# A transformer block on one core: the order of work for three engines taken from a list written in the kernel, and attention's small matmuls regrouped

## The chip, the cores and the metric

The kernel runs on one core of a Trainium2 chip. The metric is the time of one execution on the device in microseconds (us). Engines are named as in the profile: PE (TensorE) for matmuls, PEld for its weight loads, DVE (VectorE), ACT (ScalarE), POOL (GpSimd), SP (SyncE, which only issues DMAs). Each engine works through its own instructions in order.

## What is computed

A sequence of 2048 tokens of width 1024, in bfloat16, goes through an attention sublayer and a gated MLP, each behind a layer norm and with a residual. Attention has 32 heads of 32, and each token attends to 8 positions: itself and those 2, 4, ... 14 tokens earlier.

```python
h  = x + A(_layernorm(x), A_wqkv, A_wo)
h2 = h + B(_layernorm(h), B_w_in, B_w_sp, B_b_sp, B_w_out)

def A(x, wqkv, wo):              # B, S, D = x.shape; H, Dh, W, dil = 32, 32, 8, 2
    q, k, v = split(x @ wqkv)
    idx = pos[:, None] - (arange(W) * dil)[None, :]
    logits = einsum('bhsd,bhswd->bhsw', q, k[idx]) * Dh ** -0.5   # masked where idx < 0
    return einsum('bhsw,bhswd->bhsd', softmax(logits), v[idx]) @ wo

def B(x, w_in, w_sp, b_sp, w_out):    # Fh = 1792
    z = gelu(x @ w_in)
    z1, z2 = z[..., :Fh], _layernorm(z[..., Fh:])
    g = einsum('ts,bsf->btf', w_sp, z2) + b_sp[None, :, None]
    return (z1 * g) @ w_out
```

## The kernel before, in words

The tokens are cut into four chunks of 512 (`CH`), a chunk into four tiles of 128. A first phase computes, chunk by chunk, everything up to z1 and z2; a second phase (from L494 on, untouched by the change) mixes over all tokens with `w_sp` (L511), gates, and multiplies by `w_out` (L528, L536). The second phase needs z2 of all four chunks.

The first phase has, for a chunk c:

- The first layer norm: `stats` (L140 to L144) and `norm` (L162) on DVE, a square root on ACT (L157). Chunk 0 is transposed on PE (`xpose`, L170). Chunks 1 to 3 are written to DRAM (`xn_d`, L193) and come back transposed by a DMA (`xnT`, L221).
- `qkv(c)`: 192 matmuls of 128x512 on PE (L230, L238) into PSUM tiles `acc`, of which there are three; ACT copies each out (L242, L245). Chunks 1 to 3 go through DRAM (`qkv_d`) and are read back by POOL's DMAs (L257 to L259).
- `attention(c)`: head and feature lie across partitions, so the dot products run on DVE. For each of the 8 offsets w, DVE multiplies q by the shifted k (`prod`, L266), halves the 8 slices three times by adding (L268, L270, L272), and PE sums within heads by four small matmuls with a constant `E32` (L275) into one PSUM tile `L`. Then come the softmax (L280 to L291, with the exponential on ACT at L285), and four groups of eight small matmuls with a constant `B4` (L299, tile `pb`) that spread the weights back over the partitions, copied out by ACT (L300). Eight multiplications with the shifted v (L306, L309) and seven additions (L310) give `oT`.
- `b_head(c)`: for each tile, two matmuls with an identity bring the residual `xr` into PSUM (L346; not in chunk 3), 16 matmuls multiply `oT` by `wo` (L349). ACT copies out and sums for the second layer norm (L360, L361; in chunk 3 DVE does it, L354 to L358). `batch_rstd` (L313 to L326) works out mean and inverse deviation with a square root on ACT (L322). ACT normalises (L374), and a DMA transposes into `hnT` (L375); chunk 3 is transposed on PE (L384).
- `b_z2(c)`: per tile 28 matmuls (L405), gelu on ACT (L407), squares on ACT (L414), then a layer norm whose last step is on DVE (L423). `b_z1(c)`: 112 matmuls (L435) and gelu (L438).

What sets the order. The calls stand in the order qkv(0), qkv(1), attention(0), qkv(2), b_head(0), attention(1), qkv(3), b_head(1), then per chunk b_z2, b_z1, the head of the next chunk and the attention of the one after. The framework then sorts each engine's instructions by priority (the order of the code) and by when its own model finds them ready; `high_priority` blocks (L273, L284, L294) go ahead. `NWARM` = 14 matmuls on zeros (L125) run at the start while the inputs load. Tiles come from pools with a number of buffers; a new tile waits until the last reader of the buffer that it takes over is done.

## Time and profile before

| what | value |
|---|---|
| median of 6 runs | 765.97 us (762.57 to 766.83) |
| profiled execution: its time | 766.83 us |
| profiled execution: span from first to last instruction | 765.0 us |
| busy PE / DVE / ACT / POOL | 741.7 / 437.3 / 232.5 / 20.7 us |
| mean granted PE clock | 0.991 |

A row of a group reads: line, engine, operation, what it writes and reads, shape, count, then busy time in us and the mean ns of one, then the idle time of the engine just before these instructions and what ended it. Matmuls overlap in the pipeline, so the mean ns of one is longer than the distance between two. A few matmul records are missing, so counts of a group can fall short of the code's.

### The profile page before, as it was taken

The page shows a single profiled execution, that of the slowest core. Times are in us where ns is not written, and L with a number is a line of the kernel's source. Part 1 is how long each engine was busy: PE and PEld are TensorE (multiplying, and loading weights), DVE is VectorE, ACT ScalarE, POOL GpSimd, SP SyncE. Part 2 cuts the span into 40 slices and gives each one's busy share as a digit, 9 for nine tenths or more (in the row PEclk, how much of TensorE's full clock was granted, in tenths as well). Part 3 has the DMA queues.
Part 4 walks back from the last instruction along what each step waited for, and adds up shares of the span by engine and source line. Part 5 has one row for each costly group of instructions (what it writes and reads, how often), then busy time and mean ns, then how long its engine had stood idle before and what let it go on. Part 6 is the DMA issues. An engine that isn't in the chain of part 4 may idle for free.

```text
span 765.0 us, 8765 instructions
## 1 busy us (share of the span) xinstructions
PE 741.7 (97%) x3622; PEld 378.2 (49%) x3686; DVE 437.3 (57%) x445; ACT 232.5 (30%) x297; POOL 20.7 (3%) x32
## 2 busy tenths in 40 slices
PE   7999999999989998999999999999999999999997
PEld 3666666546634544444545544444444444444443
DVE  4889699989999799988945010332232222222322
ACT  3322433257328944686652562000000000000000
POOL 0000000000000000000003000000000000000000
PEclk8999999999999999999999999999999999999999
DMA  9984453174892742244047968517201711020001
GB/s 343 331 245 113 146 159 126 57 212 114 294 315 86 154 179 72 74 160 124 1 165 293 216 225 210 170 42 179 69 29 43 185 61 42 27 83 28 1 18 65
DMA packets 109640, 104.33 MB, mean 136 GB/s; under 512 B 63536, under 2 KB 87376, under 8 KB 109472
## 3 DMA queue, kind: packets, MB, share of 16 engines
q1 hardware_dynamic: 103120, 76.89, 33.4%
q0 software_dynamic: 6192, 26.36, 10.2%
q8 instruction: 29, 0.48, 0.3%
q10 hardware_dynamic: 288, 0.52, 0.2%
q14 instruction: 11, 0.09, 0.0%
HBM read 55.19 MB, written 33.88 MB: 116 GB/s over the span
## 4 chain that ended last, share of the span: by engine, by line
PE 70%; DVE 22%; ACT 4%; issue 3%; DMA 0%; DVEq 0%; ACTq 0%
PE acc L511 25%; PE acc L528 12%; PE acc L435 9%; PE acc L238 8%; PE acc L405 6%; DVE oT L310 6%; DVE prod L309 6%; PE acc L349 5%; DVE prod L266 3%; DVE scq L268 2%; PE acc L230 1%; DVE oT L306 1%; DVE scq L270 1%; PE acc L536 1%; DVE u L423 1%
## 5 line engine op out<-in xcount | busy, mean ns | idle before, releaser
L511 PE MATMUL acc<-wspT,z2sb 128*128 128x512 bf16 x878 | 193.1, 379 | 0.9
L511 PEld LDWEIGHTS <-z2sb 128*128 128x128 bf16 x896 | 87.7, 98 | 105.7
L514 DVE TENSOR_TENSOR g<-acc,bB 128x1024 bf16<-128x1024 f32 x28 | 34.3, 1225 | 159.7 <-PE acc L511 134.5
L435 PE MATMUL acc<-hnT,win 128*128 128x512 bf16 x448 | 99.6, 379 | 0.7 <-ACT z1s L438 0.7
L405 PE MATMUL acc<-win,hnT 128*128 128x512 bf16 (+1 forms) x500 | 98.1, 352 | 0.8 <-ACT u L407 0.2
L266 DVE TENSOR_TENSOR prod<-qT,kT 128x4096 bf16<-128x4096 bf16 x32 | 73.1, 2285 | 2.3 <-ACT kT L242 2.2
L405 PEld LDWEIGHTS <-hnT 128*128 128x128 bf16 x512 | 49.5, 98 | 46.6 <-issue 0.4
L435 PEld LDWEIGHTS <-win 128*128 128x128 bf16 x448 | 43.2, 98 | 50.7 <-issue 0.9
L528 PEld LDWEIGHTS <-zg 128*128 128x128 bf16 x420 | 41.1, 98 | 49.5
L309 DVE TENSOR_TENSOR prod<-vT,AB 128x4096 bf16<-128x4096 bf16 x28 | 64.2, 2291 | 1.3
L310 DVE TENSOR_TENSOR oT<-oT,prod 128x4096 bf16<-128x4096 bf16 x28 | 64.2, 2292 | 0.8
L349 PE MATMUL acc<-wo_sb,oT 128*128 128x512 bf16 x251 | 60.0, 385 | 0.5 <-issue 0.2
L245 ACT CAST stg<-acc 128x1024 bf16<-128x1024 f32 x36 | 36.4, 1013 | 77.9 <-PE acc L238 75.0
L238 PE MATMUL acc<-xnT,wv 128*128 128x512 bf16 x250 | 59.1, 388 | 0.5 <-issue 0.2
L530 DVE TENSOR_TENSOR ot<-acc,hr 128x1024 bf16<-128x1024 f32 x15 | 18.4, 1225 | 69.4 <-PE acc L528 60.5
L238 PE MATMUL acc<-xnT,wk 128*128 128x512 bf16 x252 | 56.4, 380 | 0.2
L528 PE MATMUL acc<-wout_a,zg 128*128 128x512 bf16 x236 | 54.0, 379 | 0.3
L238 PE MATMUL acc<-xnT,wq 128*128 128x512 bf16 x217 | 50.0, 380 | 0.4
L238 PEld LDWEIGHTS <-wk 128*128 128x128 bf16 x256 | 36.6, 144 | 18.2
L238 PEld LDWEIGHTS <-wv 128*128 128x128 bf16 x256 | 36.2, 145 | 18.9 <-issue 2.1
L528 PE MATMUL acc<-wout_b,zg 128*128 128x512 bf16 x175 | 40.7, 379 | 0.2
L407 ACT ACTIVATE u<-acc 128x1024 bf16<-128x1024 f32 (+1 forms) x32 | 29.3, 916 | 34.4 <-PE acc L405 34.4
(110 smaller groups left out, 535.4 us busy)
## 6 DMA issues: line engine op xcount, KB each, us to landing
qkv_d<-stg SPq DMA_DIRECT2D x36, 256.0 KB, 2.6
z_d<-z1s SPq DMA_DIRECT2D x28, 256.0 KB, 2.6
z1c<-z_d SPq DMA_DIRECT2D x28, 256.0 KB, 2.9
z_d<-u SPq DMA_DIRECT2D x12, 448.0 KB, 3.3
z2sb<-z_d POOLq DMA_DIRECT2D x12, 448.0 KB, 8.5
xr<-in_A_x_dram SPq DMA_DIRECT2D x16, 256.0 KB, 2.9
h_d<-hb SPq DMA_DIRECT2D x16, 256.0 KB, 2.8
win<-in_B_w_in_dram POOLq DMA_DIRECT2D x2, 2048.0 KB, 12.0
```

Source lines behind the costliest of these rows:

```text
L238: T.matmul(acc[:, j, :], wv[:, kt, dl, :], xnT[c][:, kt, :], start=(kt == 0), stop=(kt == KT - 1))
L245: A.copy(stg[:], acc[:])
L266: V.tensor_tensor(prod[:], qT[:], kT[:, :, o:o + CH], op=ALU.mult)
L309: V.tensor_tensor(prod[:], vT[:, :, o:o + CH], abb, op=ALU.mult)
L310: V.tensor_tensor(oT[:], oT[:], prod[:], op=ALU.add)
L349: T.matmul(acc[:, nh, :], oT[:, dl, il * P:(il + 1) * P], wo_sb[:, dl, nh * CH:(nh + 1) * CH], start=(last and dl == 0), stop=(dl == DLO - 1))
L405: T.matmul(accf[:, n0:n1], hnT[:, il, kt, :], wt[:, kt, n0:n1], start=(kt == 0), stop=(kt == KT - 1))
L407: A.activation(u[:, hf * 1024:hf * 1024 + wd], accf[:, 0:wd], ACTF.Gelu_apprx_tanh, accum_out=sums[:, il, hf:hf + 1])
L435: T.matmul(acc[:, j, :].rearrange("p (a b) -> p a b", a=TPC), wt[:, kt, f0 * P:(f0 + 1) * P], hnT[:, :, kt, :], start=(kt == 0), stop=(kt ...
L511: T.matmul(acc[:, j, :], z2sb[a][:, f * P:(f + 1) * P], wspT[:, a, :], start=(a == 0), stop=(a == NT - 1))
L514: V.tensor_tensor(g1[:], acc[:], bB[:, c * CH:(c + 1) * CH].unsqueeze(1).to_broadcast([P, 2, CH]), op=ALU.add)
L528: T.matmul(acc[:, nh, :], zg[:, f, il * P:(il + 1) * P], wt[:, f0, nh * CH:(nh + 1) * CH], start=(f == 0), stop=(f == NF - 1))
```

## The change

Everything that was called in order in the first phase is now entered as operations into a list, `Order`, each with its engine, an assumed duration, what it depends on, a priority (low goes first), and which PSUM or SBUF slots it takes and frees. `Order.run` simulates the engines, picks at each step the engine that can start earliest and on it the operation of best priority, and then emits the code in the order of the simulated starts. PE, ACT and DVE keep exactly that order (`manual_schedule`); SP and POOL are still sorted by the framework. Priorities on PE: attention's small matmuls 1, the matmuls of `head` 4, and qkv, z2 and z1 6 with a running number, so all of qkv(0) to qkv(3) comes before z2(0), z1(0), z2(1) and so on.

The work itself changes in these places:

- Attention: the second and third additions are left to PE. With `LMODE` 2 (chunks 0 and 1) one DVE addition (L270's) stays and L272's goes; with 4 (chunks 2 and 3) both go. PE sums the remaining 2 or 4 slices by accumulating matmuls of 512 or 256 columns, in 2 or 4 groups per chunk, in place of 8 groups of four with 128 columns. In the simulation every group but the last waits `LSLACK` = 1 us beyond its operands; `BSLACK` does the same for the second half of the spreading matmuls below.
- Softmax: subtraction, exponential, sum and scaling are cut into two halves. The spreading matmuls are two of 512 columns per group, with 32 rows of `B4` each, in place of eight of 128 columns; half of the groups use an `acc` buffer, and DVE copies out one of the four.
- `head`: the identity matmuls are gone. DVE adds the residual while it copies out and sums (`scalar_tensor_tensor`), ACT squares. `batch_rstd` takes the inverse root on POOL by a power of -0.5.
- z2 of chunks 0 to 2 is normalised on ACT (`Z2ACT`).
- `NWARM` is 20; x, u, stg, z1s and the normalised x share buffers (`x4k`, four of 4 KB per partition, and `xn`, six); `wo` is loaded ahead of the list; x is loaded in the same order as before.

The core of the diff:

```diff
-NWARM = 14
+NWARM = 20
+XRB = 3
+LMODE = (2, 2, 4, 4)
+LSLACK, BSLACK = 1.0, 1.0
+Z2ACT = (4, 4, 4, 0)
...
+class Order:
...
+    def add(self, eng, us, fn, deps=(), prio=5.0, lat=0.1, take=None, free=None, table=None):
+        o = _Op()
+        o.eng, o.us, o.fn, o.prio, o.lat, o.free, o.table = eng, us, fn, prio, lat, free, table
+        o.take = (take,) if isinstance(take, str) else take or ()
+        o.deps = [d if isinstance(d, tuple) else (d, d.lat) for d in deps if d is not None]
+        o.start, o.end, o.n = None, None, len(self.ops)
+        self.ops.append(o)
+        return o
...
+    def run(self):
+        left = list(self.ops)
+        while left:
+            best, cand = None, []
+            for o in left:
+                if any(d.end is None for d, _ in o.deps):
+                    continue
+                r = max([d.end + lat for d, lat in o.deps], default=0.0)
+                short = False
+                for k in o.take:
+                    if self.slots[k]:
+                        r = max(r, min(self.slots[k]))
+                    else:
+                        short = True
+                if short:
+                    continue
+                cand.append((max(r, self.clock.get(o.eng, 0.0)), o))
+            assert cand, "nothing can start"
+            first = {}
+            for t, o in cand:
+                if o.eng not in first or t < first[o.eng]:
+                    first[o.eng] = t
+            eng = min(first, key=lambda e: first[e])
+            mine = [(o.prio, t, o.n, o) for t, o in cand if o.eng == eng and t <= first[eng] + 0.02]
+            late = [(o.prio, t, o.n, o) for t, o in cand if o.eng == eng and t > first[eng] + 0.02]
+            pick = min(mine, key=lambda x: x[:3])
+            for x in sorted(late):
+                if x[0] < pick[0] - 0.5 and x[1] < pick[1] + 0.3 * pick[3].us:
+                    pick = x
+                    break
+            _, t, _, o = pick
+            if o.table and o.table != self.table:
+                t += 1.28
+                self.table = o.table
+            o.start, o.end = t, t + o.us
+            if o.eng in self.clock:
+                self.clock[o.eng] = o.end
+            for k in o.take:
+                self.slots[k].remove(min(self.slots[k]))
+            if o.free:
+                self.slots[o.free].append(o.end + 0.1)
+            left.remove(o)
+        self.ops.sort(key=lambda o: (o.start, o.n))
+        for o in self.ops:
+            o.fn()
...
+    nhalf = cpool.tile([P, TPC], FP32, name="nhalf")
+    V.memset(nhalf[:], -0.5)
...
+            pairs[i // 2] = l1.tile([P, 2, D], BF16, name="xp", tag="x4k", bufs=4)
+        xts[i] = pairs[i // 2][:, i % 2, :]
...
+    warm = l1.tile([P, CH], BF16, name="warm", tag="xn", bufs=6)
+    V.memset(warm[:], 0.0)
...
-    for c in range(1, NCH):
-        for i in range(c * TPC, (c + 1) * TPC):
-            stats(V, i)
-        rstd_of(c * TPC, (c + 1) * TPC)
-        for i in range(c * TPC, (c + 1) * TPC):
-            xn = norm(i)
-            dma(xn_d[c][(i - c * TPC) * P:(i - c * TPC + 1) * P, :], xn[:])
...
+    o_ = Order({"PE": 12.9, "ACT": 12.0, "DVE": 12.6, "POOL": 12.0}, {"acc": 3, "L": 1, "prod": 2, "part": 2})
+    add = o_.add
...
+    X_AT = {1: 18.5, 2: 27.5, 3: 30.5}
+    xn_ready = {}
+
+    def ln1(c):
+        sts = []
+        for i in range(c * TPC, (c + 1) * TPC):
+            arrive = add("DMA", X_AT[c] + 0.8 * (i % TPC), lambda: None)
+            sts.append(add("DVE", 1.40, lambda i=i: stats(V, i), [arrive], prio=2.0))
+        def sq():
+            G["sd", c] = l1.tile([P, TPC], FP32, name="sd1", tag="sd1")
+            A.activation(G["sd", c][:], mv1[:, c * TPC:(c + 1) * TPC, 1], ACTF.Sqrt, bias=eps_t[:])
+        s1 = add("ACT", 0.25, sq, sts, prio=1.0, table="sqrt")
+        r1 = add("DVE", 0.15, lambda: V.reciprocal(rstd1[:, c * TPC:(c + 1) * TPC], G["sd", c][:]), [s1], prio=1.0)
+        ns = []
+        for il in range(TPC):
+            def nrm(i=c * TPC + il, il=il):
+                xn = norm(i)
+                dma(xn_d[c][il * P:(il + 1) * P, :], xn[:])
+            ns.append(add("DVE", 0.48, nrm, [r1], prio=1.5))
+        def tr():
+            xnT[c] = xtp.tile([P, KT, CH], BF16, name="xnT", tag="xnT")
+            nc.sync.dma_start_transpose(xnT[c][:], xn_d[c].rearrange("s (a p) -> s a p", p=P))
+        G["xnT", c] = dma_op(10.0, tr, ns + ([G["qkvlast", c - 2]] if c >= 2 else []))
...
+                        stg = l1.tile([P, 2, CH], BF16, name="stg", tag="xn", bufs=6)
+                        A.copy(stg[:], G[key][:])
+                        dma(qkv_d[xi][:, 2 * dp:2 * dp + 2, c * CH:(c + 1) * CH], stg[:])
+                G["ev", c, xi, dp] = add("ACT", 0.93, ev, [last], prio=2.0, free="acc", lat=0.15)
...
+        mode = LMODE[c]
+        nw = 8 // mode
...
+                def qk(w=w, wi=wi, o=o, g=g):
+                    st = qs[w]
+                    qT, kT, _ = att_in[c]
+                    if wi == 0:
+                        parts[g] = att.tile([P, nw, mode, CH], BF16, name="part", tag="part", bufs=2)
+                    st["prod"] = att.tile([P, DLO, CH], BF16, name="prod", tag="prod", bufs=2)
+                    V.tensor_tensor(st["prod"][:], qT[:], kT[:, :, o:o + CH], op=ALU.mult)
+                def add1(g=g, wi=wi, w=w):
+                    p_ = qs[w]["prod"]
+                    dst = parts[g][:, wi] if mode == 4 else p_[:, 0:4, :]
+                    V.tensor_tensor(dst, p_[:, 0:4, :], p_[:, 4:8, :], op=ALU.add)
+                def add2(g=g, wi=wi, w=w):
+                    p_ = qs[w]["prod"]
+                    V.tensor_tensor(parts[g][:, wi], p_[:, 0:2, :], p_[:, 2:4, :], op=ALU.add)
+                pr_ = prev = add("DVE", 2.21, qk, [d_q, d_k, (prev, 0.0) if prev else None, first], prio=3.0, take=("prod", "part") if wi == 0 else "prod")
+                pr_ = add("DVE", 1.15, add1, [pr_], prio=3.0, free="prod" if mode == 4 else None)
+                if mode == 2:
+                    pr_ = add("DVE", 0.60, add2, [pr_], prio=3.0, free="prod")
+                first = None
+                adds.append(pr_)
...
+            slack = add("DMA", LSLACK if g < W_WIN // nw - 1 else 0.0, lambda: None, adds)
+            def lm(g=g):
+                if g == 0:
+                    st["L"] = ps_att.tile([P, W_WIN, P], FP32, name="L", tag="L")
+                L = st["L"]
+                for z in range(mode):
+                    for sq in range(4):
+                        T.matmul(L[32 * sq:32 * sq + 32, nw * g:nw * g + nw, :], E32,
+                                 parts[g][:, :, z, sq * P:(sq + 1) * P],
+                                 start=(z == 0), stop=(z == mode - 1), tile_position=(0, 32 * sq))
+            lms.append(add("PE", 0.6, lm, [slack], prio=1.0, take="L" if g == 0 else None, free="part", lat=0.2))
...
+                def pbm(sh=sh, ws=ws, hw=hw):
+                    if sh == 0:
+                        pb = ps_att.tile([P, 2, 4, P], FP32, name="pb", tag="L")
+                    else:
+                        pb = ps_acc.tile([P, 2, 4, P], FP32, name="pba", tag="acc")
+                    st["pb", hw, sh] = pb
+                    for j in range(2):
+                        sq = 2 * sh + j
+                        T.matmul(pb[:, j], B4[32 * sq:32 * sq + 32, :], st["attn"][32 * sq:32 * sq + 32, ws, :],
+                                 start=True, stop=True, tile_position=(32 * sq, 0))
+                pm = add("PE", 0.25, pbm, [wait], prio=1.0, take="acc" if sh else "L", lat=0.2)
+                eng = "DVE" if (hw == 0 and sh == 1) else "ACT"
+                def cp(sh=sh, ws=ws, hw=hw, eng=eng):
+                    (V.tensor_copy if eng == "DVE" else A.copy)(
+                        st["AB"][:, ws, sh * 256:(sh + 1) * 256].rearrange("p w (j s) -> p j w s", j=2), st["pb", hw, sh][:])
+                abs_[hw, sh] = add(eng, 1.14 if eng == "DVE" else 0.95, cp, [pm], prio=1.0 if eng == "ACT" else 2.9,
+                                   free="acc" if sh else "L", lat=0.15)
...
+        s1 = add("DVE", 0.75, a1, deps, prio=prio)
+        s2 = add("POOL", 1.4, lambda: nc.gpsimd.tensor_tensor(G[key]["rstd"][:], G[key]["var"][:], nhalf[:], op=ALU.pow), [s1], lat=0.4)
...
-            if not last:
-                for nh in range(2):
-                    T.matmul(acc[:, nh, :], ident, xr[:, nh * CH:(nh + 1) * CH], start=True, stop=False)
...
+            def res(il=il, i=i):
+                hb = st["hnc"][:, il, :]
+                V.scalar_tensor_tensor(hb, st["acc", il][:].rearrange("p a b -> p (a b)"), 1.0, st["xr", il][:],
+                                       op0=ALU.mult, op1=ALU.add, accum_out=st["hsum"][:, il:il + 1])
+                dma(h_d[i * P:(i + 1) * P, :], hb)
+            r_ = add("DVE", 1.23, res, [m_] + ([G["hdone", c - 1]] if c else []), prio=1.0, free="acc", lat=0.15)
+            def hsq(il=il):
+                A.activation(st["xr", il][:], st["hnc"][:, il, :], ACTF.Square, accum_out=st["hsq"][:, il:il + 1])
+                if il + XRB < TPC:
+                    xr_load(il + XRB)
+            sqd.append(add("ACT", 1.12, hsq, [r_], prio=3.0, lat=0.25))
...
+            nd.append(add("DVE", 0.5, nrm, [rs], prio=0.6) if last else add("ACT", 1.16, nrm, [rs], prio=4.0))
+        G["hdone", c] = nd[-1]
...
+            n_ = add("ACT", 1.75, nrm, [rs], prio=5.5) if Z2ACT[c] > il else add("DVE", 0.62, nrm, [rs], prio=2.5)
...
-    qkv(1)
-    attention(0)
-    qkv(2)
-    b_head(0)
-    attention(1)
-    qkv(3)
-    load_win(0, wtile([P, KT, 1024], "win0", "wA"))
-    load_win(1, wtile([P, KT, 768], "win1", "wA"))
-    load_win(2, wtile([P, KT, 1024], "win2", "wB"))
-    b_head(1)
...
+    for c in range(1, NCH):
+        ln1(c)
+        qkv(c)
+
+    def open_():
+        load_win(2, wtile([P, KT, 1024], "win2", "wB"))
+        t1.close()
+        pools["bq"] = t2.enter_context(tc.tile_pool(name="bq", bufs=1))
+        load_win(3, pools["bq"].tile([P, KT, 768], BF16, name="win3"))
+
     t2 = ExitStack()
-    bq = t2.enter_context(tc.tile_pool(name="bq", bufs=2))
+    G["win", 0] = dma_op(10.0, lambda: load_win(0, wtile([P, KT, 1024], "win0", "wA")), [G["wdone", 3, 0]])
+    G["win", 1] = dma_op(10.0, lambda: load_win(1, wtile([P, KT, 768], "win1", "wA")), [G["wdone", 3, 1]])
+    G["open"] = dma_op(0.0, open_, [G["qkvlast", 3], G["ev", 3, 2, 3]])
+    G["win", 2] = dma_op(10.0, lambda: None, [G["open"]])
+    G["win", 3] = dma_op(14.0, lambda: None, [G["open"]])
...
+        attention(c)
+        if c < NCH - 1:
+            head(c)
+    for c in range(NCH - 1):
         b_z2(c)
-        if c == 0:
-            load_win(3, bq.tile([P, KT, 768], BF16, name="win3", bufs=1))
-        Z1SPLIT = {1: 0, 2: 3}.get(c, 0)
-        if Z1SPLIT:
-            b_z1(c, 0, Z1SPLIT)
-        if 0 < c and c + 1 < NCH:
-            fin = b_head(c + 1)
-        if c + 1 == NCH - 1:
-            att_stack.close()
-            zpool = ctx.enter_context(tc.tile_pool(name="z2sb", bufs=1, side="right"))
-            for i in range(NT):
-                z2sb[i] = zpool.tile([P, FH], BF16, name=f"z2sb{i}")
-            for i in range((NCH - 1) * TPC):
-                dma_w(z2sb[i][:], z2_d[i * P:(i + 1) * P, :])
-            wsp0_inst = load_wsp(0)
-            ps_tp2 = ctx.enter_context(tc.tile_pool(name="ps_tp2", bufs=2, space=PSUM))
-            fin()
-        last_store = b_z1(c, Z1SPLIT)
-        if c + 1 == NCH - 1:
-            tc.add_manual_dep(wsp0_inst.ins, last_store.ins.name,
-                              mybir.DependencyInfo(mybir.DependencyClass.NoSync, mybir.DependencyReason.DATA),
-                              reason="keep the xbar transpose out of the z1 store stream")
-        if c + 2 < NCH:
-            attention(c + 2)
+        b_z1(c)
...
+    head(NCH - 1)
+    dma_op(0.0, zload, [G["hdone", NCH - 1]])
+    b_z2(NCH - 1)
+    b_z1(NCH - 1)
...
+    with tc.manual_schedule(engines={mybir.EngineType.PE, mybir.EngineType.Activation, mybir.EngineType.DVE}):
+        o_.run()
```

507 lines of the change are left out of this document (296 added, 211 removed).

## The prediction

> **What bounds the kernel now.** I read the page first, then busy time by stretches, then PE's own waits and timeline.
>
> ```profile
> span 765.0 us, 8765 instructions
> PE 741.7 (97%) x3622; PEld 378.2 (49%) x3686; DVE 437.3 (57%) x445; ACT 232.5 (30%) x297; POOL 20.7 (3%) x32
> ...
> DVE  4889699989999799988945010332232222222322
> ```
>
> PE is busy for 97% of the span; DVE, in fortieths of it, is nearly full in the first half and idle later. So the question is what PE does besides the matmuls that the result needs. The chain of waits gives the unit:
>
> ```profile
> 446.29 24.17 PE acc L435 x112
> 470.46 0.22 PE acc L511
> ```
>
> 112 matmuls of 128x512 in 24.17 us are 0.2158 us each. The second phase starts at 470.46 and with its tail takes 765.0 - 470.46 = 294.5 us; the change leaves it alone. PE's timeline has the first useful matmul:
>
> ```profile
> 1.19 5.99 PE L125 MATMUL wps<-warm 128*128 128x512 bf16 x14 [1.19 <-DVE eps_t L91]
> ...
> 12.66 1.47 PE L230 MATMUL acc<-xnT,wq 128*128 128x512 bf16 x3 [0.88 <-DVE xnT L171]
> ```
>
> From 12.66 to 470.46 are 457.8 us. The first phase needs 768 (qkv) + 256 (wo) + 448 (z2, counted in 512 columns) + 448 (z1) = 1920 matmuls, 414.3 us. The other 43.5 us are what a better order or less side work could win. They are made of small groups, waits and clock:
>
> ```profile
> 61.21 4.32 PE L238 MATMUL acc<-xnT,wq 128*128 128x512 bf16 x19
> 65.46 0.24 PE L275 MATMUL L<-part,csb 128*32 128x128 bf16 x4
> 65.63 1.73 PE L238 MATMUL acc<-xnT,wq 128*128 128x512 bf16 x7
> ...
> 92.16 1.25 PE L238 MATMUL acc<-xnT,wv 128*128 128x512 bf16 x5
> 93.47 0.61 PE L299 MATMUL pb<-attn,csb 128*128 128x128 bf16 x8
> 93.91 1.47 PE L238 MATMUL acc<-xnT,wv 128*128 128x512 bf16 x6
> ...
> 95.74 1.25 PE L238 MATMUL acc<-xnT,wv 128*128 128x512 bf16 x4
> ```
>
> ```profile
> L238 PE MATMUL acc<-xnT,wk 128*128 128x512 bf16 x252 | 56.4, 380 | 0.2
> L346 PE MATMUL acc<-xr,csb 128*128 128x512 bf16 x22 | 7.3, 402 | 0.0
> L384 PE MATMUL tp<-csb,hnc 128*128 128x128 bf16 x32 | 2.3, 219 | 0.0
> ```
>
> The last matmul of a run begins one duration (0.38) before the run ends: 65.15, and the next full one at 65.63. That is 0.48 where plain matmuls are 0.22 apart: an L group costs 0.26, 32 of them 8.3 us. The same for pb: 93.03 to 93.91 and 95.00 to 95.74, less 0.22 each, 0.66 and 0.52, mean 0.59, times 16 is 9.4 us. The 24 identity matmuls (22 recorded) are 5.2 us by the unit, chunk 3's transposes 2.3 us.
>
> ```profile
> 6.90:10.30 3.40, 1.59 (x22) 1.13 (x21) 3.36 (x15) 1.63 (x5) 0.00 (x0) 1.00 1.05 395
> 10.30:13.70 3.40, 2.52 (x19) 1.69 (x16) 1.06 (x2) 2.17 (x3) 0.00 (x0) 0.50 1.05 388
> 13.70:17.10 3.40, 3.18 (x9) 1.32 (x8) 0.00 (x0) 0.00 (x0) 0.00 (x0) 0.50 1.05 387
> ...
> 133.20:136.60 3.40, 1.34 (x10) 0.94 (x10) 3.37 (x4) 0.27 (x1) 0.00 (x0) 1.00 0.26 90
> 136.60:140.00 3.40, 3.40 (x9) 1.33 (x8) 3.40 (x4) 0.13 (x1) 0.00 (x0) 0.50 0.00 0
> ...
> 218.50:221.90 3.40, 3.40 (x10) 1.18 (x8) 3.37 (x4) 2.12 (x4) 0.00 (x0) 0.50 0.99 393
> ```
>
> In these stretches (span, PE busy, ..., clock in the third column from the end) the clock is 0.5 from 10.3 to 17.1, which loses (17.1 - 12.66)/2 = 2.2 us of useful work, and twice more for 3.4 us, 1.7 us each: 5.6 together. Here a stretch with 1.34 us busy is followed by a slow one. [...]
>
> The ledger: 12.66 + 414.3 + 8.3 + 9.4 + 5.2 + 2.3 + 5.6 + 294.5 = 752.3; the remaining 12.7 us are waits. Most are named:
>
> ```profile
> PE L L275 <- DVE part L272: 7.1, 6, 2.2
> PE pb L299 <- DVE attn L291: 3.0, 3, 1.0
> ```
>
> **The change, part by part.** *Identity matmuls*: 5.2 us leave PE for good. In exchange DVE has 12 more passes like L354's, below.
>
> *L groups*: a group is now eight matmuls of 512 columns or sixteen of 256, four side by side on 32 columns of the array each, as the four of L275 are (all four in 0.24). Streaming is 2 x 0.2158 = 0.43 or 4 x 0.108 = 0.43; the old group streamed 0.05 of its 0.26, so 0.21 is entry and exit: 0.64 per group. Two groups in each of two chunks and four in each of the others are 12, 7.7 us. No gain here, 0.6 us.
>
> *pb groups*: two matmuls of 512 columns on different 32 rows. Side by side 0.22 + 0.21 = 0.43 each, 6.9 us for 16; one after the other 0.64, 10.2 us. The nearest row is L275's, tiled matmuls side by side, so 6.9: 2.5 us gained, between -0.8 and 2.5. [...]
>
> *Warm-up*: six more matmuls on zeros run until about 8.5 at full clock, before the transposes (from 8.96), so nothing is pushed. They fill the stretch from 6.9, which had 1.59 busy. The next stretch keeps its 2.52 and may fall as before. Bounds for the cold loss: 0 and 2.2; I take 1.5, since only one of the two stretches changes.
>
> *Order*: 12.7 us of waits and the 3.4 us of clock that followed two of them. PE's queue is fixed, so a small matmul whose operands are late holds everything behind it. The list keeps an early chunk's big matmuls as cover and puts the L groups 1 us behind their operands, except the last of a chunk; the first half's pb groups have no slack either. The assumed durations can be checked: 1.727 for eight matmuls is 8 x 0.2158, and a product of 2.21 against
>
> ```profile
> 53.92 2.28 DVE L266 TENSOR_TENSOR prod<-qT,kT 128x4096 bf16<-128x4096 bf16 x1
> 56.12 0.42 DVE L272 TENSOR_TENSOR part<-scq 128x512 bf16<-128x512 bf16 x1
> ```
>
> 2.20 from start to start. So drift should stay below the slack, and what is left are the 12 places without slack, at a third of a microsecond: 4 us of waits, none long enough for the clock. Bounds: 0, and the old 12.7 + 3.4.
>
> *DVE as supplier.* Attention ran from 43.74 (chunk 0's first product) to the end of the last addition, 382.46: 338.7 us.
>
> ```profile
> 43.74 2.29 DVE L266 TENSOR_TENSOR prod<-qT,kT 128x4096 bf16<-128x4096 bf16 x1 [2.20 <-ACT kT L242]
> ...
> 380.17 2.29 DVE L310 TENSOR_TENSOR oT<-oT,prod 128x4096 bf16<-128x4096 bf16 x1
> ```
>
> ```profile
> L270 DVE TENSOR_TENSOR scq<-scq 128x1024 bf16<-128x1024 bf16 x32 | 22.1, 692 | 0.9
> L272 DVE TENSOR_TENSOR part<-scq 128x512 bf16<-128x512 bf16 x32 | 13.4, 418 | 0.3
> L354 DVE TENSOR_TENSOR hb<-acc,xr 128x1024 bf16<-128x1024 f32 x4 | 4.9, 1225 | 8.4 <-PE acc L349 8.4
> L423 DVE TENSOR_SCALAR u<-u,l3mean,l3rstd 128x1792 bf16<-128x1792 bf16 x12 | 8.1, 739 | 0.0
> ```
>
> Gone: 13.4 + 11.0 (half of L270) + 5.4 (two chunks of L423). Added: 12 x 1.225 = 14.7, and four copies of pb, 4.9. DVE's waits for the exponential and the spread weights were 9.4 + 7.0:
>
> ```profile
> DVE ssum L287 <- ACT scq L285: 9.4, 4, 3.4
> DVE oT L306 <- ACT AB L300: 7.0, 4, 1.9
> ```
>
> Halving should hide half, 8. Net -18: attention ends at about 364. PE would then have z1 of chunk 2 ahead until 12.66 + 1632 x 0.2158 + about 20 (groups, clock, waits) = 385, so chunk 3's head finds cover. The tightest place is chunk 2: attention(3) takes a quarter of the 320, less 2.8 as it drops both additions, so attention(2) ends near 364 - 77 = 287. Its head (64 matmuls, 13.8) ends at 301, and `hnT` is there some 24 later by my estimate (10.9 of transpose below, the rest for residuals, statistics, POOL's power and four normalisations among ACT's other work): 325. PE arrives at 12.66 + 1408 x 0.2158 + 15 = 331. Covered by 6 us; each microsecond beyond that is lost.
>
> ```profile
> win<-in_B_w_in_dram POOLq DMA_DIRECT2D x2, 2048.0 KB, 12.0
> ...
> hnT<-hnc SPq DMA_TRANSPOSE x3, 10.9
> ```
>
> POOL's power replaces the ACT root; no row shows one. The nearest is the page's POOL mean, 20.7/32 = 0.65 us; I take twice that, and it lies under the 6 us as long as no load waits ahead of it in POOL's queue. The loads of `w_in` follow the last qkv on that queue: the second pair has 24 us of z2 as cover against 12.0 to land. On SP, `wo` (2 MB) is now ahead of the first layer norm's stores, 6 us at the 347 GB/s moved then, and normalised tile 10 waits for tile 4's store, whose buffer it takes; the transposes of `xnT` stand on SP behind those stores.
>
> ```profile
> 12.60:43.70 31.10, 30.71 (x131) 19.52 (x135) 19.64 (x47) 8.79 (x11) 0.00 (x0) 0.93 0.97 347
> ```
>
> That may start attention(0) up to 6 us late and show once as a PE wait at its first L group; it is inside the bound of the waits. ACT loses L360 and the root's table loads and gains z2; at 30% it bounds nothing.
>
> Sum: 12.66 + 414.3 + 7.7 + 6.9 + 2.3 + 1.5 + 4 + 294.5 = 743.9 us of span. The profiled run took 766.83 for its span of 765.0 (+1.8), and the median of six is 0.9 below that run: 743.9 + 0.9 = 744.8, so **745**.
>
> **The rivals.** *Waits move, and don't shrink.* PE waits of the old size at other places, 16.1 in place of 4: 757. For it: each chunk still has a softmax in which PE's small groups depend on DVE; against it: the measured durations in the list.
>
> *Slower: the fixed order stalls PE at every group.* If DVE runs d late at each of the 28 groups, the time is 741 + 28 d. It passes 769.8 (before plus 0.5%, about what a measurement can tell from no change) from d = 1.04; at 1.2, about half a product, it is 774. For it: the longest old wait was 2.2, and a group of four offsets needs four products. Against: a wait puts PE behind the list, which makes the next one shorter, and only 9 of 48 groups waited before.
>
> *DVE becomes the bound, and the change brings nothing.* If attention keeps its old pace and the added passes come on top, it ends at 382.5 + 14.7 = 397.2. Then follow head 3 (13.8), its norm and transposes, z2 and z1 (224 matmuls, 48.3) and the second phase:
>
> ```profile
> 404.73 1.67 PE L349 MATMUL acc<-wo_sb,oT 128*128 128x512 bf16 x7
> ...
> 413.73 1.52 DVE L385 COPY hnT<-tp 128x1024 bf16<-128x1024 bf16 x2
> ```
>
> 406.4 to 415.25 is 8.8: 397.2 + 13.8 + 8.8 + 48.3 + 294.5 + 0.9 = 763.5. Against it: 24.4 us of additions really go.
>
> **How the numbers follow.** Forecast 0.66, waits move 0.18, DVE bound 0.08, slower 0.08. The forecast's own range is 740 to 750 (waits 0 to 9). The range reaches from 738 (no wait, no cold clock, pb groups without the drain) to 757, the second case. Faster by over 0.5% (below 762.1) takes the first two cases: 0.84; the same 0.08; slower 0.08.
>
> **What would show it.** Right: no matmuls with `xr`; phase two beginning near 449; PE's waits for DVE at the L and pb groups under 5 us together; a clock of 1.0 after 20 us; attention's last addition near 364. Wrong: a gap of PE before z2 of chunk 2; waits at every L group; pb groups near 0.64; a first product later than 47.

## The result, and the profile after

The changed kernel takes 741.77 us (median of 8 runs, 741.59 to 742.06), the kernel before 764.49 us (median of 16). The ratio is 0.9704, with a 95% interval of 0.9687 to 0.9720: 22.7 us faster. The prediction was 745 (738 to 757), and faster. Where the longest run of a kernel lies more than 1.5% above its shortest, the ratios below leave it out and the medians do not.

The profiled execution took 742.06 us for a span of 740.3. The top of its page, with the PE, DVE and clock rows in fortieths of the span and the shares of the chain that ended last:

```profile
PE 725.4 (98%) x3542; PEld 369.3 (50%) x3604; DVE 421.3 (57%) x419; ACT 220.9 (30%) x270; POOL 37.0 (5%) x40
...
DVE  4889699988999799979943012221232223212222
...
PEclk9999999999999999999999999999999999999999
...
PE 85%; DVE 10%; ACT 2%; issue 1%; POOL 1%; DMA 1%; POOLq 0%; DVEq 0%; ACTq 0%
```

PE is busy for 16 us less than before, in a span that is 25 us shorter, and its clock is full throughout (1.00 on average). DVE is still nearly full in the first half. The chain still passes through DVE for a tenth of the span, which the share of busy time does not tell.

PE's waits from the first useful matmul to the border of the phases (what waits, what it waits for, then us in total, times, longest) and, from PE's timeline, the first useful matmul, an L group, a pair of spreading groups, and the border of the two phases:

```profile
PE acc L540 <- DVE oT L498: 1.2, 1, 1.2
PE pb L471 <- ACT AB L476: 1.1, 2, 0.9
...
PE tp L580 <- DVE hnT L582: 1.0, 1, 1.0
```

```profile
13.01 2.32 PE L337 MATMUL acc<-xnT,wq 128*128 128x512 bf16 x9 [1.17 <-ACT xnT L251]
...
57.69 3.83 PE L346 MATMUL acc<-xnT,wq 128*128 128x512 bf16 x17
61.45 0.62 PE L423 MATMUL L<-part,csb 128*32 128x512 bf16 x8
62.00 2.16 PE L346 MATMUL acc<-xnT,wq 128*128 128x512 bf16 x9
...
171.46 1.89 PE L346 MATMUL acc<-xnT,wk 128*128 128x512 bf16 x7
173.28 0.39 PE L471 MATMUL pb<-attn,csb 32*128 32x512 bf16 x2
173.29 0.39 PE L471 MATMUL pba<-attn,csb 32*128 32x512 bf16 x2
173.61 1.95 PE L346 MATMUL acc<-xnT,wk 128*128 128x512 bf16 x8
...
445.54 4.70 PE L760 MATMUL acc<-wspT,z2sb 128*128 128x512 bf16 x20
```

No row of the waits names an L group any more. An L group: the last full matmul ahead of it begins 0.38 before 61.52, at 61.14, the next at 62.00, so 0.86 - 0.22 = 0.64 as forecast. Two neighbouring spreading groups (four matmuls) run all at once: 172.97 to 173.61 is 0.64 - 0.22 = 0.42 for both, where 0.43 had been forecast for each. Chunks 1 and 3 have two such pairs each. In chunks 0 and 2 three groups run together and the fourth comes alone, after waits of 0.9 and 0.3 for ACT's copy out of the PSUM buffer that it takes over. With these the ledger of the prediction can be filled in (us; the pb groups are counted as eight pairs of 0.42; the waits are what is left over, and 3.3 of the 4.8 have a row above):

| part | before | predicted | after |
|---|---|---|---|
| up to the first useful matmul | 12.66 | 12.66 | 13.01 |
| 1920 matmuls | 414.3 | 414.3 | 414.3 |
| L groups | 8.3 | 7.7 | 7.7 |
| pb groups | 9.4 | 6.9 | 3.4 |
| identity matmuls | 5.2 | 0 | 0 |
| chunk 3's transposes | 2.3 | 2.3 | 2.3 |
| slow clock | 5.6 | 1.5 | 0 |
| waits in the first phase | 12.7 | 4 | 4.8 |
| second phase and tail | 294.5 | 294.5 | 294.8 |
| span | 765.0 | 743.9 | 740.3 |

Counted from the timeline group by group, the pb groups are about 3.8 and the waits then 4.4.

So of 24.7 us of span, 13.5 came from waits and clock (7.9 + 5.6), 6.0 from the spreading groups, 5.2 from the identity matmuls and 0.6 from the L groups, less 0.6 at the start and in the tail. The execution of the kernel before that this ledger takes apart is the longest of the sixteen, 2.3 above their median, so 2.0 of the 24.7 belong to it alone. Its mean clock was 0.991, while shorter ones show up to 0.998, so those 2.0 lie most likely in its slow clock. Which edit moved the waits the ledger can't say; that was tried on the chip.

### The profile page after: what moved, and what is told of

The parts are those of the page before. It is cut to its first block, busy times and chain, and to the rows that moved or that the text cites. A ratio compares the mean times of both kernels' runs of the same rounds, so it can differ in the third digit from the quotient of the medians.

```text
span 740.3 us, 8543 instructions
## 1 busy us (share of the span) xinstructions
PE 725.4 (98%) x3542; PEld 369.3 (50%) x3604; DVE 421.3 (57%) x419; ACT 220.9 (30%) x270; POOL 37.0 (5%) x40
## 4 chain that ended last, share of the span: by engine, by line
PE 85%; DVE 10%; ACT 2%; issue 1%; POOL 1%; DMA 1%; POOLq 0%; DVEq 0%; ACTq 0%
PE acc L760 26%; PE acc L346 18%; PE acc L777 12%; PE acc L613 9%; PE acc L663 8%; PE acc L540 7%; DVE prod L492 4%; DVE oT L498 4%; PE acc L337 1%; PE L L423 1%; PE acc L785 1%; DVE oT L489 1%; DMA xp<-in_A_x_dram 1%; ACT u L642 0%; ACT z1s L669 0%
## 5 line engine op out<-in xcount | busy, mean ns | idle before, releaser
L613 PE MATMUL acc<-win,hnT 128*128 128x512 bf16 (+1 forms) x501 | 97.1, 352 | 0.6 <-issue 0.2
L613 PEld LDWEIGHTS <-hnT 128*128 128x128 bf16 x512 | 49.8, 98 | 46.8 <-issue 0.7
L400 DVE TENSOR_TENSOR prod<-qT,kT 128x4096 bf16<-128x4096 bf16 x32 | 72.2, 2283 | 0.0
L498 DVE TENSOR_TENSOR oT<-oT,prod 128x4096 bf16<-128x4096 bf16 x28 | 64.0, 2285 | 0.1
L540 PE MATMUL acc<-wo_sb,oT 128*128 128x512 bf16 x249 | 56.1, 379 | 1.6 <-DVE oT L498 1.2
L346 PE MATMUL acc<-xnT,wv 128*128 128x512 bf16 x250 | 56.0, 379 | 0.5 <-issue 0.2
L346 PEld LDWEIGHTS <-wv 128*128 128x128 bf16 x256 | 36.6, 144 | 18.9 <-issue 0.7
L540 PEld LDWEIGHTS <-oT 128*128 128x128 bf16 x256 | 24.7, 98 | 31.9 <-DVE oT L498 2.2
```

Of the source, the lines that this page charges most:

```text
L346: T.matmul(G[key][:, j, :], wv[:, kt, dl, :], xnT[c][:, kt, :], start=(kt == 0), stop=(kt == KT - 1))
L400: V.tensor_tensor(st["prod"][:], qT[:], kT[:, :, o:o + CH], op=ALU.mult)
L498: prev = add("DVE", 2.21, lambda w=w: V.tensor_tensor(oTs[c][:], oTs[c][:], pvs[w][:], op=ALU.add), [prev, m_], prio=3.0, lat=0.15, free=" ...
L540: T.matmul(st["acc", il][:, nh, :], oTs[c][:, dl, il * P:(il + 1) * P], wo_sb[:, dl, nh * CH:(nh + 1) * CH], start=(dl == 0), stop=(dl == ...
L613: T.matmul(accf[:, n0:n1], hnTs[c][:, il, kt, :], wins[hf][:, kt, n0:n1], start=(kt == 0), stop=(kt == KT - 1))
```

## The experiments

The theory was the prediction's: the written order takes the waits and the clock losses that follow them, the smaller work comes on top, and DVE as supplier has some microseconds in hand. The rivals: that the lighter work alone did it, in any order; that DVE's relief did it; or that warm-up and clock did. Every kernel but before_warm20 is the changed one with one edit.

**The order left to the framework**

```diff
-    with tc.manual_schedule(engines={mybir.EngineType.PE, mybir.EngineType.Activation, mybir.EngineType.DVE}):
-        o_.run()
+    o_.run()
```

> The changed kernel with the same list and the same emission, but PE, ACT and DVE sorted by the framework again. If the fixed order is what removed the waits of PE, some 9 us of waits come back and perhaps a slow clock after two of them: 750 to 754 us. If the gain comes from the work that was taken off PE and the emission alone is order enough, 742 to 744.

Measured: 758.94 us (757.18 to 761.33), ratio to before 0.9906 (0.9879 to 0.9934). That is 17.2 us above the changed kernel, more than either case that was expected. PE's waits in its profile:

```profile
PE acc L540 <- DVE hb L549: 4.7, 3, 2.5
PE acc L540 <- ACT z1s L669: 2.4, 1, 2.4
...
PE pba L471 <- ACT z1s L669: 1.6, 1, 1.6
PE acc L613 <- DMA hnT<-hb: 1.5, 1, 1.5
```

They are not at the L groups: PE waits for the copy that frees a buffer of `acc` (`hb`, `z1s`) and for the transpose `hnT`. Behind the first useful matmul the rows of the first phase come to 14.4, against 3.3 in the changed kernel. Part of the rest is clock: 0.58 and 0.50 in the two stretches from 10.3 to 17.1, and 0.990 on average. The new work with the framework's order keeps only 5.6 of the 22.7 us, so the change needs the written order for most of its gain, though the parts need not add up: DVE's residual, which is new, is what PE waits for most here.

**Warm-up**: 14 matmuls in the changed kernel, 20 in the kernel before.

```diff
-NWARM = 20
+NWARM = 14
```

> The changed kernel with 14 warm-up matmuls again. If the six extra ones are what keeps PE's clock at 1.0 from the start, PE is idle again from about 7.2 to 9.5 us, the clock falls to 0.5 for one or two stretches of 3.4 us, and the time is 743.3 to 744.0 us, 1.5 to 2.2 more than the 741.8 of the changed kernel. If the clock at the start came from elsewhere (where the first stretch falls in the run), 741.8.

Measured: 744.04 us (742.48 to 745.12), ratio 0.9718 (0.9694 to 0.9741): 2.3 above the changed kernel. Busy time and clock (third column from the end) in stretches at the start, first with 14 and then with 20:

```profile
6.90:10.30 3.40, 1.28 (x13) 1.28 (x14) 3.36 (x15) 1.24 (x6) 0.00 (x0) 0.79 1.05 386
10.30:13.70 3.40, 2.53 (x24) 2.31 (x23) 1.12 (x2) 2.64 (x3) 0.00 (x0) 0.71 1.05 388
```

```profile
6.90:10.30 3.40, 2.35 (x20) 1.13 (x18) 3.40 (x14) 1.65 (x7) 0.00 (x0) 1.00 1.05 378
10.30:13.70 3.40, 2.15 (x27) 1.77 (x26) 1.52 (x4) 2.66 (x3) 0.00 (x0) 1.00 1.05 391
```

Two stretches with 2.35 and 2.15 us busy kept the full clock; one with 1.28 fell to 0.79 on average and the next to 0.71. The busy time of such a stretch does not settle it alone. With 20 matmuls the stretch from 6.9 has 1.37 us busy in pb_in_line and 1.58 in root_on_act, and the clock stays at 1.00; it has 1.18 in framework_order, and 0.58 follows; in the kernel before it had 1.59, and 0.50 followed. So stretches with 1.18 to 1.59 of 3.4 us busy, like the one with 1.34 that the prediction has ahead of a slow one, came before a slow one in some executions and not in others.

```diff
-NWARM = 14
+NWARM = 20
```

> The kernel before with 20 warm-up matmuls and nothing else. If they keep the clock up, the 2.2 us of useful work lost between 12.66 and 17.1 come back, and nothing behind depends on the start: 762.0 to 763.0 against 764.5. If the later waits swallow the earlier start (attention starts earlier but the waits for DVE only grow), 764.5.

Measured: 763.10 us (761.83 to 767.19), ratio 0.9986 (0.9964 to 1.0008): 1.3 less, no difference that stands out. In its profiled execution (761.83) the clock stays full from 5.2 us on, and the waits at the L groups are 7.2 as before. Its ten runs reach from a clock of 1.000 (761.83) to 0.991 (767.19), so even with 20 matmuls the clock varies from run to run there. So the warm-up is worth about 2 us in the changed kernel and no more than that in the one before; it is not what made the change.

**L groups: two or four slices in all chunks**

```diff
-LMODE = (2, 2, 4, 4)
+LMODE = (2, 2, 2, 2)
```

> LMODE 2 in all four chunks: DVE gets 16 additions of 0.69 us more (11.0 us), PE four L groups of 0.64 less (2.6 us). If DVE's supply is used up at chunk 3's head (PE already waits 1.2 us there for the last addition), nearly all of the 11 us shows: 748 to 751 us, with PE's wait at the head near 11. If PE alone sets the time and the cover of 12 us that the prediction worked out is there, 739.

Measured: 757.61 us (754.79 to 766.85), ratio 0.9884 (0.9841 to 0.9928). That is slower than either case that was expected, and the wait is not at chunk 3's head, where it was expected: there PE waits 0.7. At the L groups PE waits once, in attention of chunk 3 (PE's timeline, then the stretches that follow):

```profile
322.25 5.35 PE L663 MATMUL acc<-hnT,win 128*128 128x512 bf16 x24
336.47 1.04 PE L423 MATMUL L<-part,csb 128*32 128x512 bf16 x8 [8.86 <-DVE part L407]
337.44 0.61 PE L613 MATMUL acc<-win,hnT 128*128 128x512 bf16 x1
```

```profile
334.40:337.80 3.40, 1.33 (x9) 0.27 (x9) 2.22 (x4) 0.00 (x0) 0.00 (x0) 0.50 0.51 96
337.80:341.20 3.40, 3.18 (x8) 1.21 (x8) 3.27 (x5) 1.65 (x3) 0.00 (x0) 0.50 0.00 0
```

Between 327.6 and 336.5 nothing runs, and 1.33 and 3.18 us of work follow at half speed. The row names DVE's last addition, since the L group stands first in PE's queue. What stands behind it, z2 of chunk 2 (L613), would not have run either. SP's timeline and the landing time of `hnT`, in this kernel and, below it, SP's in the changed one:

```profile
329.82 4.82 SPq L587 DMA_TRANSPOSE hnT<-hb  x1
```

```profile
DMA to landing us min/median/max: 6.7/6.7/6.7
```

```profile
320.29 5.23 SPq L587 DMA_TRANSPOSE hnT<-hb  x1
```

`hnT` of chunk 2 is there at 329.82 + 6.7 = 336.5, the very time at which the L group's operands are. So DVE is late for both: with 0.69 us more for each of chunk 2's eight offsets and for the first of chunk 3's, the chain behind it moved by 9.5 us, and PE ran out of z1 to do. The profiled execution (754.97) is 12.9 above the changed kernel's; 8.9 are this wait and about 3 the slow clock behind it (0.50 for those 4.51 us of work, 0.81 for the next 3.4 us). It is the place that the prediction called tightest, chunk 2's head and z2. The single late group of the slower rival it is not: the work behind it was not ready.

```diff
-LMODE = (2, 2, 4, 4)
+LMODE = (4, 4, 4, 4)
```

> LMODE 4 in all chunks: DVE loses 16 additions of 0.69 us (11.0 us), PE gets four more L groups of 0.64 (2.6 us). If DVE's lateness costs only the 1.2 us at chunk 3's head, that goes and 2.6 come: 743.0 to 743.5. If DVE sets more of the time than that one wait shows, under 740.

Measured: 744.23 us (743.79 to 744.63), ratio 0.9724 (0.9703 to 0.9745): 2.5 above the changed kernel, the 4 x 0.64 = 2.6 of four more groups. The relief of DVE bought nothing: attention ends at 361.5, 13.5 us earlier, and PE's wait at chunk 3's head fell from 1.2 to 0.3, but the wait for that chunk's transposes rose from 1.0 to 1.5 and one of 0.5 appeared at chunk 2's head. The chosen (2, 2, 4, 4) is best of the three.

**Slack**

```diff
-LSLACK, BSLACK = 1.0, 1.0
+LSLACK, BSLACK = 0.0, 0.0
```

> LSLACK and BSLACK 0: the eight L groups and eight pb groups that stood 1 us behind their operands in the list stand right behind them. If the slack is what absorbs drift, each group waits some tenths, together 2 to 5 us, and the time is 743.5 to 747. If the list is accurate enough without it, 741 to 742.5.

Measured: 741.80 us (741.63 to 742.01), ratio 0.9693 (0.9672 to 0.9714): no change, as its second case said. The slack is not what keeps the waits away.

**Identity matmuls**, first or last in a tile; in both DVE adds the residual as well, so it counts twice.

```diff
+                        if not last:
+                            for nh in range(2):
+                                T.matmul(st["acc", il][:, nh, :], ident, st["xr", il][:, nh * CH:(nh + 1) * CH], start=True, stop=False)
...
-                                     start=(dl == 0), stop=(dl == DLO - 1))
+                                     start=(last and dl == 0), stop=(dl == DLO - 1))
```

> The 24 identity matmuls are back in the heads of chunks 0 to 2, and DVE still adds, so the residual is added twice in those rows; the list is told 0.43 us per tile. If PE's time is the sum of its own work, 5.2 us more, less the wait of 1.2 at chunk 3's head that the later PE absorbs: 745.8 to 747.0. If they lie beside waits on DVE that PE has anyway, under 743.

Measured: 752.96 us (752.81 to 753.07), ratio 0.9836 (0.9816 to 0.9856): 11.2 above the changed kernel, more than twice what was expected. The rest is a new wait:

```profile
PE acc L540 <- DMA xr<-in_A_x_dram: 6.0, 3, 2.7
```

`xr` has three buffers (`XRB`), so a chunk's fourth tile is loaded only when ACT has squared the first; in each of three chunks the matmuls now wait for that. To tell the work from the wait, the same matmuls were put last:

```diff
-                                     start=(dl == 0), stop=(dl == DLO - 1))
+                                     start=(dl == 0), stop=(last and dl == DLO - 1))
+                    if half == 1 and not last:
+                        for nh in range(2):
+                            T.matmul(st["acc", il][:, nh, :], ident, st["xr", il][:, nh * CH:(nh + 1) * CH], start=False, stop=True)
```

> The 24 identity matmuls again, but as the last of their tile in place of the first, with DVE adding too (the residual comes in twice in chunks 0 to 2). With them first the time was 752.96, 11.2 above the changed kernel: by my reading 5.2 of work and 6.0 of PE waiting for the loads of xr. If so, the wait goes and the work stays: 746.0 to 747.5. If the 11.2 came from the work and the order of the list that it shifts, it stays at 751 to 753.

Measured: 746.75 us (746.63 to 746.91), ratio 0.9761 (0.9736 to 0.9786): 5.0 above the changed kernel. So about 5 us is the price of the 24 matmuls, and 6 of ident_back's 11.2 were the wait.

**Spreading matmuls one after the other** (all on the first 32 rows, with the first slice's weights in place of each one's own)

```diff
-                        T.matmul(pb[:, j], B4[32 * sq:32 * sq + 32, :], st["attn"][32 * sq:32 * sq + 32, ws, :],
-                                 start=True, stop=True, tile_position=(32 * sq, 0))
+                        T.matmul(pb[:, j], B4[0:32, :], st["attn"][0:32, ws, :],
+                                 start=True, stop=True, tile_position=(0, 0))
```

> The spreading matmuls all read rows 0 to 31 in place of four different sets of 32 rows, so the weights are those of the first 128 tokens of each chunk and the output is not the reference's; counts and sizes are the same. If the four matmuls of two neighbouring groups run side by side only because their rows differ, each pair of groups streams 0.86 in place of 0.22: 8 pairs by 0.64 is 5.1 us of PE, of which some lies in waits: 744 to 747. If they were not side by side, no change: 741.8.

Measured: 744.55 us (744.32 to 744.70), ratio 0.9728 (0.9703 to 0.9753): 2.8 above the changed kernel. The same place in its timeline:

```profile
171.65 1.89 PE L346 MATMUL acc<-xnT,wk 128*128 128x512 bf16 x7
173.47 0.60 PE L471 MATMUL pb<-attn,csb 32*128 32x512 bf16 x2
173.91 0.59 PE L471 MATMUL pba<-attn,csb 32*128 32x512 bf16 x2
174.44 1.95 PE L346 MATMUL acc<-xnT,wk 128*128 128x512 bf16 x8
```

173.16 to 174.44, less 0.22, is 1.06 for the four, against 0.42 on different rows. Eight pairs would make 5.1; 2.3 of it came back, 1.6 as shorter waits elsewhere (for `oT` 1.2 to 0.5, for `AB` 1.1 to 0.2).

**Softmax in one piece**

```diff
-        for hw in range(2):
-            ws = slice(4 * hw, 4 * hw + 4)
+        for hw in range(1):
+            ws = slice(0, 8)
```

(and so for the sum and the scaling, with one pass of eight offsets in place of two of four)

> Subtraction, exponential, sum and scaling of the softmax whole again in place of halves; the spreading matmuls stay as changed. The prediction counted 8 us of DVE waits saved by the halves. If that were so, attention ends 8 us later, PE runs out of cover at the heads of chunks 2 and 3, and the time is 747 to 752. If the halves only replace one wait by another, as the trace after suggests (its softmax stretches are not shorter than before), 741 to 743.5.

Measured: 759.13 us (756.96 to 771.31), ratio 0.9913 (0.9880 to 0.9946), far outside both cases that were expected. The profiled execution is the longest of the four, 29.2 above the changed kernel's; the other three are 15 to 19 above its median. Attention's last addition ends at 377.1, only 2.1 later than in the changed kernel (374.98). DVE's busy time over attention in the kernel before, the changed kernel and this one (span, PE busy, PEld busy, DVE busy):

```profile
43.74:382.46 338.72, 325.65 (x1688) 180.82 (x1716) 313.55 (x253) 175.47 (x223) 11.48 (x13) 0.99 0.47 143
```

```profile
44.76:374.98 330.22, 326.10 (x1675) 178.35 (x1700) 303.40 (x239) 175.59 (x205) 25.29 (x19) 1.00 0.50 154
```

```profile
44.76:377.10 332.34, 327.32 (x1681) 178.82 (x1705) 301.99 (x224) 176.45 (x202) 23.33 (x19) 1.00 0.50 154
```

Without the halves DVE is busy 1.4 less and idle 3.5 more (30.3 against 26.8). So halving hides 3.5 us, not 8, and costs 1.4. Most of the 29.2 us is elsewhere, at the start of the second phase:

```profile
472.73 0.58 PE L758 MATMUL acc<-wspT,z2sb 128*128 128x512 bf16 x1 [23.45 <-DMA wspT<-in_B_w_sp_dram]
```

`wspT` is `w_sp`, loaded and transposed by a DMA on SP's queue. SP's timeline (start, duration) and the time from issue to landing of its four loads, here and in the changed kernel:

```profile
396.10 64.21 SPq L678 DMA_TRANSPOSE wspT<-in_B_w_sp_dram  x1
```

```profile
DMA to landing us min/median/max: 9.5/12.5/76.5
```

```profile
395.75 20.30 SPq L680 DMA_TRANSPOSE wspT<-in_B_w_sp_dram  x1
```

```profile
DMA to landing us min/median/max: 10.4/11.6/23.9
```

396.1 + 76.5 = 472.6 is when PE goes on. Issued at the same time, the load took three times as long. The other three runs have no trace; that they too waited there is likely, but was not seen. What differs in the queues is the start of the twelve loads of `z2sb` on POOL's, which the last section takes up.

**All four copies of the spread weights on ACT**

```diff
-                eng = "DVE" if (hw == 0 and sh == 1) else "ACT"
+                eng = "ACT"
```

> All four copies of the spread weights on ACT, none on DVE. DVE loses 4 passes of 1.22 us and 4.1 us of waits for PE ahead of them, but its first product with v waits for ACT's second copy. If DVE's supply costs 1.2 us at chunk 3's head and little else, 740.3 to 741.2, a version below both kernels. If ACT's copies come one after the other and hold DVE and the PSUM buffer longer, 742 to 744.

Measured: 749.32 us (742.83 to 763.83), ratio 0.9787 (0.9734 to 0.9841). Even the shortest run is above the changed kernel, so the hoped-for gain is not there. The profiled execution of 744.11 has no such gap, but `wspT` took 51.0 us: 394.93 + 51.0 = 445.9, and PE reached for it at 447.6. With 1.7 us in hand there, a load a few microseconds later would already hold PE up, which may explain the scatter of the other runs; that they waited there was not seen.

**The root on ACT**

```diff
-        s2 = add("POOL", 1.4, lambda: nc.gpsimd.tensor_tensor(G[key]["rstd"][:], G[key]["var"][:], nhalf[:], op=ALU.pow), [s1], lat=0.4)
+        s2 = add("ACT", 0.25, lambda: A.activation(G[key]["rstd"][:], G[key]["var"][:], ACTF.Sqrt), [s1], prio=0.5, table="sqrt")
```

(with DVE's reciprocal behind it)

> The inverse root by a square root on ACT and a reciprocal on DVE in place of POOL's power. POOL took 1.0 to 3.0 us for it and DVE waited 5.1 us in all. ACT then loads a table for the root and one for what follows, 2 x 1.28 for each of 8 roots, 20 us of ACT, which is idle for two thirds. If only DVE's wait matters, no change or up to 1 us less: 740.8 to 742. If the table loads delay the copies out of PSUM that PE needs, 743 to 746.

Measured: 742.98 us (742.84 to 743.66), ratio 0.9713 (0.9689 to 0.9738): 1.2 above the changed kernel, between the two cases that were expected. POOL's power is the better of the two, by little.

No kernel beat the changed one; the one without slack equals it.

## Why the prediction was right, step by step

The forecast case held: the time is 3.2 below 745, inside the range and the case's own 740 to 750. The ledger gives the terms.

*Right.* The identity matmuls (5.2 forecast, 5.0 by ident_last). The L groups (0.64 each in the trace, and 2.5 for four more by four_slices). The second phase, whose 294.5 became 294.8. DVE's work: 29.8 gone and 19.6 added makes 10.2 less, and its busy time over attention fell by 313.55 - 303.40 = 10.15. That is closer than the terms were, since the 1.4 that the halving costs was not among them. That no wait would stand at the L groups, also right.

*Right by luck.* The size of the waits, 4 forecast and 4.8 left. They were forecast as a third of a microsecond at each of the 12 places without slack. None of those has a row; the rows are the head and the transposes of chunk 3 and the fourth spreading group behind ACT's copy.

*Sizes that were off.* The pb groups: 16 x 0.43 = 6.9 became 3.4 to 3.8, since the list puts two groups in a row and all four matmuls run side by side; the forecast took only the two of one group together. The range's lower end, 738, takes 0.8 us off the pb groups as the share of a drain; no run shows such a term, and what the runs showed is the 0.42 of two groups together. The cold clock: 1.5 became 0. The forecast had the second stretch fall as before, and it did not, nor in any traced run with 20 matmuls but framework_order. The first useful matmul came 0.35 later. Together with 0.8 more of waits and 0.3 in the tail: -3.5 - 1.5 + 0.35 + 0.8 + 0.3 = -3.55, from 743.9 to 740.3.

*DVE as supplier: the step that failed.* Attention was to end at 364 and ended at 374.98. The prediction had named 364 as one of its signs of being right. Attention began 1.0 later; the other 10 are its idle time, 25.2 before and 26.8 after where 17.2 was forecast. DVE's waits within attention:

```profile
DVE ssum L444 <- ACT sme L441: 7.5, 4, 2.3
DVE ssum L432 <- PE L L423: 4.4, 3, 2.4
DVE AB L476 <- PE pba L471: 4.1, 4, 1.4
DVE L L428 <- PE L L423: 2.0, 1, 2.0
DVE l2nb L515 <- POOL l2rstd L512: 1.8, 2, 0.9
DVE oT L489 <- ACT AB L476: 1.4, 2, 1.0
...
DVE l3nb L515 <- POOL l3rstd L512: 0.9, 1, 0.9
```

For the exponential and the spread weights they are 7.5 + 4.1 + 1.4 = 13.0 where 16.4 stood: 3.4 saved, not 8, and whole_softmax says the same (3.5). Against that stand 6.4 for the L groups, which had cost DVE 2.7:

```profile
DVE mx L280 <- PE L L275: 2.4, 3, 1.7
...
DVE L L278 <- PE L L275: 0.3, 1, 0.3
```

Ahead of the maximum DVE now waits for a whole group of eight or sixteen matmuls and not for four short ones, and PE comes to it behind big matmuls; that this is the reason was not tested. POOL's power costs 2.7 where the root on ACT had cost 1.1, and the residual's passes, which are new, wait 1.6.

*Covers.* A cover is work that PE can do while it would otherwise wait for DVE. The prediction gave chunk 3's head 385 - 364 = 21 us of it (the text ahead of two_slices says 12, which is not what the prediction works out). Attention ended 11 late. PE's timeline shows that some cover was still left when PE waited 1.2 at the head:

```profile
375.04 13.99 PE L540 MATMUL acc<-wo_sb,oT 128*128 128x512 bf16 x62 [1.16 <-DVE oT L498]
388.86 5.34 PE L663 MATMUL acc<-hnT,win 128*128 128x512 bf16 x24
```

24 matmuls of z1 of chunk 2, 5.2 us, stand behind the head in the list, where they cover its norm. With those PE would have come to the head at 379, so 4 us of the 21 were left. How much of a delay of DVE shows there is not settled: with attention 2.1 later (whole_softmax) the waits for the head and the transposes behind it are 3.2 together in place of 2.2, with attention 13.5 earlier (four_slices) 1.8. At z2 of chunk 2 it had `hnT` at 325 and PE at 331. `hnT` came at 320.29 + 6.7 = 327 and PE at 329.6: 3 us of cover in place of 6, no wait, and in two_slices, 9.5 us later, the wait of 8.9. By two_slices the rival in which DVE becomes the bound was nearer than its chance of 0.08 says.

*A reason that was wrong.* The slack was to absorb the drift of the list against the chip. Without it nothing changes. What framework_order and two_slices point to is which big matmuls stand ahead of the dependent ones, and how far DVE's chain is ahead of PE; the margin of a microsecond isn't it.

*A place that was left out.* The second phase was costed as untouched. Its work is, but the loads ahead of it (`z2sb`, `wspT`) were moved with the list, onto queues that the framework sorts. Their time held in the changed kernel, with 445.5 - (395.75 + 23.9) = 26 us to spare, and not in whole_softmax. In that execution it cost 23.5 us of waiting, a rival that the prediction did not see.

Open: how the 13.5 us of waits and clock split between the written order and the lighter work. framework_order has the new work without the order; no run has the order with the old work.

## What to carry to other kernels

A written order pays when enough independent big matmuls stand ahead of whatever depends on the slower engine; here it had one or two places where that cover is thin, and making the supplier a little slower finds them (0.7 us per offset became a wait of 8.9 us), while the average busy time does not. Splitting the softmax to overlap it hid 3.5 us of the waits for its steps where 8 were counted, while DVE's waits for the L groups grew from 2.7 to 6.4, so a saving is counted once per engine's idle time and not per row. When the order upstream changes, look also at when the transfers of the next phase are issued: over the kernels here the slowest landing of `wspT` lay between 10.2 and 76.5 us.

## What the runs showed of the hardware

*A transposing load beside plain ones.* How long after the first load of `z2sb` (POOL's queue) the first transpose of `wspT` (SP's queue) is issued, the median landing of the twelve `z2sb` loads, and the slowest landing of `wspT`, each from the timelines and tile views of the profiled executions:

| kernel | issued later by | `z2sb` lands in | `wspT`, slowest |
|---|---|---|---|
| four_slices | 27.1 us | 9.7 | 10.2 |
| before | 16.7 | 8.5 | 12.3 |
| root_on_act | 7.9 | 8.5 | 18.9 |
| after | 6.2 | 9.5 | 23.9 |
| framework_order | 6.0 | 9.1 | 22.2 |
| two_slices | 4.5 | 17.6 | 35.1 |
| act_copies | 4.5 | 22.7 | 51.0 |
| whole_softmax | 4.5 | 30.0 | 76.5 |

The profiled executions that the table leaves out fit in: no_slack, pb_in_line and warm14 at 6.2 (`wspT` 22.5 to 23.8), ident_last at 10.5 (18.8), ident_back and before_warm20 at 16.6 and 16.7 (12.5 and 11.5). At 4.5 us both kinds of load take about 1.5 to 3.2 times as long as at 6.2, and by an amount that varies. The three kernels at 4.5 are those whose runs scatter by more than 10 us. The first load of `z2sb` starts when POOL has waited for chunk 3's head, and the transposed load stands behind z1's stores, so their distance moves with the order upstream. No run changed this distance alone, so it is not shown to be the cause, and why 4.5 and 6.2 differ so much was not found out.

*POOL's power beside DVE.* The power of 128x4 values was forecast at 1.3 us. In the changed kernel it took from 1.03 to 2.99. POOL's timeline, and DVE's at both places:

```profile
228.66 2.99 POOL L512 TENSOR_TENSOR l2rstd<-l2var,nhalf 128x4 f32<-128x4 f32 x1 [22.69 <-DVE l2var L510]
...
244.15 1.03 POOL L512 TENSOR_TENSOR l3rstd<-l3var,nhalf 128x4 f32<-128x4 f32 x1 [0.18 <-DVE l3var L510]
```

```profile
228.49 2.28 DVE L400 TENSOR_TENSOR prod<-qT,kT 128x4096 bf16<-128x4096 bf16 x1
```

```profile
244.53 1.23 DVE L432 TENSOR_REDUCE ssum<-L 128x128 f32<-128x1024 f32 x1 [0.46 <-PE L L423]
```

Beside a product of two tiles in SBUF, POOL ends 0.9 after the product does (230.77 to 231.65), as if it had begun then; beside a reduction that reads PSUM it takes its 1.03. Of the changed kernel's other six, the four that begin beside a DVE pass over two operands in SBUF (L404 twice, L400, L498) took 1.92 to 2.89 and ended 0.87 to 0.89 after that pass, and the two that ran while DVE stood idle took 1.03. What holds POOL back there no run shows.

*Small matmuls on different rows.* Four matmuls of 32 rows and 512 columns into two PSUM tiles took 0.42 us together with entry and exit in the changed kernel, and 1.06 on the same rows in pb_in_line.
